# Earlier value casts, whole matmul pieces per step, earlier softmax sums and wider-spread exponentials in a fused attention and expert kernel

## The chip, the cores and the metric

One core of one Trainium2 chip. The metric is device time in microseconds (us) of one execution. Executions of one kernel mostly lie within 1% of each other; jobs run on different chips, so a variant is compared with the runs of the kernel before from its own job. Engines in the profile: PE is TensorE, PEld its weight loads, DVE VectorE, ACT ScalarE, POOL GpSimd, SP SyncE.

## The reference

Two parts. A linear attention over 8 batches, 8 heads, 576 tokens and 64 columns, whose result is 4608 tokens of 512 columns; then a mixture of experts that sends each token to the expert with the largest logit.

```python
def _attn_ref(q, k, v):
    q_s = softmax over the head columns of q          # cut: max, exp, sum, divide
    k_s = softmax over the tokens of k                # cut
    kv = np.einsum('bhsd,bhse->bhde', k_s, v)
    return np.einsum('bhsd,bhde->bhse', q_s, kv)

def _moe_ref(x, modality_id, w_gate, modality_bias, w1, w2):
    logits = x @ w_gate + modality_bias[modality_id]
    e_idx = np.argmax(logits, axis=1)
    gate_w = softmax(logits)[np.arange(N), e_idx]     # cut
    for e in range(E):
        mask = e_idx == e
        h = np.maximum(x[mask] @ w1[e], 0.0)
        out[mask] = gate_w[mask, None] * (h @ w2[e])
```

With these inputs the bias decides the expert, so tokens fall to two experts, one per modality. The kernel computes with those two and has a loop behind it for the case that they are not enough.

## The kernel before

Per batch, TensorE makes 36 kv matmuls from exp(k) and v, transposes exp(q), and makes the logits; VectorE turns the logits into an expert per token (the routing chain); matmuls with a permutation put the scaled tokens, sorted by expert, into `xs`. Between these small dependent steps TensorE is fed with *pieces* of the expert layers (the FFN): 8 matmuls of 256 columns (h) or 4 of 512 (y). The generator of a batch yields a number at each place where there is time for pieces, and `weave` hands them out; at some steps it also issues one ScalarE exponential or GpSimd cast of the next batch:

```python
def weave(side, rate, preps=(), at=()):
    owed = 0.0
    preps = iter(preps)
    for i, x in enumerate(side):
        if i in at:
            next(preps, None)          # one exponential or v cast of the next batch
        owed += x * rate
        while owed >= 1:
            mains(1)                   # one FFN piece
            owed -= 1
    alone(preps)
```

The end of the routing chain, with the softmax sums between the permutation and the scaling of the tokens:

```python
def route(b):
    ...                                 # logits, maximum, exp -> pr (ScalarE), isa, pos
    xps = [x_tile(b, 0)]
    yield 0.8
    xps.append(x_tile(b, 1))
    yield 1.6
    r_ps = ...                          # 2 matmuls with isa: ranks of the tokens
    ...                                 # aoff, pos
    nc.vector.tensor_tensor(out=perm, in0=iota_row.., in1=pos.., op=ALU.is_equal)
    ...
    gsum = small.tile([P, NT], FP32, name="gsum")
    nc.vector.reduce_sum(out=gsum, in_=pr, axis=AX.X)
    nc.vector.tensor_scalar_add(out=gsum, in0=gsum, scalar1=1e-9)
    nc.vector.reciprocal(out=gsum, in_=gsum)
    nc.vector.tensor_tensor(out=qi, in0=qi, in1=gsum.., op=ALU.mult)
    scale(0)                            # x_sb = x_ps * qi
    scale(1)
    yield 3.3
    ...                                 # xT: permutation matmuls, ScalarE copies into xs
```

The row numbers of the output are made by two routines: `slots(b)` makes the one-hot tiles `hlo` (VectorE) and `hv` (GpSimd by default), `places(b)` multiplies them (the `id` matmuls) and forms the row numbers `ix`. The results of an FFN piece go out by an indirect store on GpSimd's queue; the first ones are held until row numbers exist. The passage into batch 2, which the argument is about:

```python
    p2 = prep(2, nc.gpsimd)        # exp of k, casts of v (on GpSimd), exp of q, two steps each
    for i in range(6):
        mains(1)
        if i == 2:
            places(0)
            hold[0] = False
            store_held()           # the held stores enter GpSimd's queue here
        next(p2)

    def batch(b):
        side = chain(attend(b), route(b))
        for i, x in enumerate(side):
            if i == 0:
                slots(b - 1)
            if i == 5:
                places(b - 1)
            yield x
```

The softmax here doesn't subtract the row's maximum and nothing guards it: scores larger than these inputs give would overflow.

## Time and profile before

| | before |
|---|---|
| median (range) | 228.09 us (227.97 to 228.23), 3 runs |
| span of the profiled execution | 226.6 us |
| TensorE busy | 192.5 us, 85% |
| mean granted clock of TensorE | 0.971 |
| dearest wait of TensorE after the start | 3.5 us, for GpSimd's cast of batch 2's v |
| half clock in mid-span | 6.83 us, from 56.7 to 63.5 |

### The profile page before, as it was taken

The page shows a single profiled execution, that of the slowest core. Times are in us where ns is not written, and L with a number is a line of the kernel's source. Part 1 is how long each engine was busy: PE and PEld are TensorE (multiplying, and loading weights), DVE is VectorE, ACT ScalarE, POOL GpSimd, SP SyncE. Part 2 cuts the span into 40 slices and gives each one's busy share as a digit, 9 for nine tenths or more (in the row PEclk, how much of TensorE's full clock was granted, in tenths as well). Part 3 has the DMA queues.
Part 4 walks back from the last instruction along what each step waited for, and adds up shares of the span by engine and source line. Part 5 has one row for each costly group of instructions (what it writes and reads, how often), then busy time and mean ns, then how long its engine had stood idle before and what let it go on. Part 6 is the DMA issues. An engine that isn't in the chain of part 4 may idle for free.

```text
span 226.6 us, 5272 instructions
## 1 busy us (share of the span) xinstructions
PE 192.5 (85%) x1963; PEld 138.3 (61%) x1982; DVE 147.9 (65%) x499; ACT 150.9 (67%) x238; POOL 75.0 (33%) x86
## 2 busy tenths in 40 slices
PE   0287888985899998999999999999998999999940
PEld 0276775773666576567866876687677648476610
DVE  7788978986238784968687797868759766211100
ACT  3979698989173799489759958976553946244310
POOL 8910330004733461049015603810630071240350
PEclk9999999999589999999999999999999999999995
DMA  6999999999999949932983101120210022130220
GB/s 210 371 392 394 401 398 394 389 391 392 402 396 397 378 151 387 395 114 56 350 316 143 48 3 46 46 95 0 97 73 24 0 95 93 46 142 0 83 107 1
DMA packets 18953, 46.55 MB, mean 205 GB/s; under 512 B 1245, under 2 KB 1245, under 8 KB 18926
## 3 DMA queue, kind: packets, MB, share of 16 engines
q1 hardware_dynamic: 15936, 36.70, 43.7%
q0 software_dynamic: 2960, 9.44, 10.9%
q8 instruction: 16, 0.26, 0.5%
q14 instruction: 11, 0.09, 0.1%
q10 hardware_dynamic: 30, 0.05, 0.1%
HBM read 36.75 MB, written 9.70 MB: 205 GB/s over the span
## 4 chain that ended last, share of the span: by engine, by line
PE 61%; DVE 20%; ACT 5%; issue 4%; DMA 4%; POOL 1%; SPq 0%; POOLq 0%; ACTq 0%; DVEq 0%
PE y_ps L758 23%; PE h_ps L739 20%; PE xT_ps L631 4%; DMA st<-in_v_dram 4%; PE tp_ps L429 4%; PE x_ps L521 3%; PE kv_ps L392 3%; DVE lg L555 2%; PE lg_ps L491 2%; DVE x_sb L589 1%; ACT ek L374 1%; DVE lw L505 1%; DVE qi L503 1%; DVE perm L608 1%; PE id_ps L689 1%
## 5 line engine op out<-in xcount | busy, mean ns | idle before, releaser
L786 POOL DMA_INDIRECT out_dram<-y_sb,ix x37 | 37.0, 1000 | 127.5 <-DVE ix L703 32.9
L739 PE MATMUL h_ps<-xs,W 128*128 128x256 bf16 x576 | 70.0, 272 | 0.0
L758 PE MATMUL y_ps<-W,hT 128*128 128x512 bf16 x269 | 68.4, 383 | 1.8 <-ACT W L356 0.7
L739 PEld LDWEIGHTS <-W 128*128 128x128 bf16 x576 | 53.7, 98 | 7.1
L750 ACT ACTIVATE hT<-h_ps 128x512 bf16<-128x512 f32 x70 | 40.2, 605 | 13.0 <-PE h_ps L739 8.4
L644 ACT CAST xs<-xT_ps 128x512 f32 (+2 forms) x80 | 38.9, 556 | 8.3 <-PE xT_ps L631 7.8
L758 PEld LDWEIGHTS <-hT 128*128 128x128 bf16 x296 | 27.0, 98 | 26.4 <-issue 1.7
L589 DVE TENSOR_TENSOR x_sb<-x_ps,qi 128x512 bf16<-128x512 f32 (+1 forms) x40 | 26.2, 683 | 5.8 <-PE x_ps L521 5.3
L356 ACT COPY y_sb<-y_ps 128x512 f32<-128x512 f32 x22 | 13.0, 590 | 24.6 <-PE y_ps L758 23.8
L356 DVE COPY y_sb<-y_ps 128x512 f32<-128x512 f32 x14 | 9.7, 691 | 22.8 <-PE y_ps L758 18.9
L392 PE MATMUL kv_ps<-vb,ek 64*128 64x129 bf16 x288 | 12.7, 251 | 13.3 <-DVE vb L356 9.8
L392 PEld LDWEIGHTS <-ek 64*128 64x128 bf16 x288 | 10.7, 111 | 14.7 <-ACT ek L374 9.8
L374 ACT ACTIVATE ek<-st 128x1152 bf16<-128x1152 f32 x16 | 18.5, 1176 | 0.2 <-DMA st<-in_k_dram 0.2
L374 ACT ACTIVATE eq<-st 128x1152 bf16<-128x1152 f32 x16 | 18.2, 1190 | 0.1
L631 PEld LDWEIGHTS <-x_sb 128*128 128x128 bf16 (+1 forms) x160 | 11.0, 100 | 10.3 <-DVE x_sb L589 3.3
L521 PE MATMUL x_ps<-kvbd,et 128*128 128x128 bf16 (+1 forms) x160 | 16.9, 232 | 0.0
L631 PE MATMUL xT_ps<-perm,x_sb 128*128 128x128 bf16 (+1 forms) x160 | 15.3, 219 | 1.8 <-DVE x_sb L589 1.6
L429 PE MATMUL tp_ps<-ident,eq 128*128 128x128 bf16 x144 | 13.8, 243 | 0.7 <-ACT eq L374 0.5
L429 PEld LDWEIGHTS <-eq 128*128 128x128 bf16 x144 | 11.5, 112 | 3.8 <-issue 0.9
L356 POOL CAST vb<-st 128x1152 bf16<-128x1152 f32 x12 | 13.4, 1144 | 0.0
L521 PEld LDWEIGHTS <-et 128*128 128x128 bf16 (+1 forms) x160 | 11.4, 106 | 2.3 <-issue 1.7
L356 ACT COPY et<-tp_ps 128x1024 bf16<-128x1024 bf16 x7 | 7.2, 1028 | 6.2 <-PE tp_ps L429 6.1
(153 smaller groups left out, 219.3 us busy)
## 6 DMA issues: line engine op xcount, KB each, us to landing
st<-in_k_dram SPq DMA_DIRECT2D x8, 1152.0 KB, 12.8
st<-in_moe_w_dram SPq DMA_DIRECT2D x8, 1024.0 KB, 13.7
st<-in_v_dram SPq DMA_DIRECT2D x6, 1152.0 KB, 9.6
st<-in_q_dram SPq DMA_DIRECT2D x6, 1152.0 KB, 8.8
st<-in_v_dram SPq DMA_DIRECT2D x4, 576.0 KB, 8.0
st<-in_q_dram SPq DMA_DIRECT2D x4, 576.0 KB, 12.0
out_dram<-y_sb,ix POOLq DMA_INDIRECT x37, 3.3
W<-in_moe_modality_id_dram ACTq DMA_DIRECT2D x1, 36.0 KB
```

The costliest lines, as they stand in the source:

```text
L356: return (nc.scalar.copy if eng is nc.scalar else eng.tensor_copy)(out=out, in_=in_)
L374: nc.scalar.activation(out=view((eks if nm == "k" else eqs)[b], [[Dh, 2], [HG * Dh, NJ], [1, Dh]], 2 * g * Dh), in_=src[:, 2 * g : 2 * g + ...
L392: nc.tensor.matmul(out=kv[hg][:, 130 * hp : 130 * hp + 129], lhsT=ek[rows, j, P * hp : P * hp + P], rhs=vb[rows, j, hp, 0:129], start=(j = ...
L429: nc.tensor.transpose(out=view(tp[c0], [[2 * nj * 64, 2], [1, 64]], hp * nj * 64 + jj * 64), in_=eq[:, c0 + jj, P * hp : P * hp + P], iden ...
L521: nc.tensor.matmul(out=view(x_ps, [[2 * Dh, 2], [1, Dh]], (4 * (p_ % 2) + p_ // 2) * Dh, (0, T)), lhsT=et[:, p_, tcol[t] : tcol[t] + T], r ...
L589: scaled[b] = nc.vector.tensor_tensor(out=view(x_out[t], [[2 * Dh, HG], [Dh, 2], [1, Dh]], 0, (0, T)), in0=view(xps[t], [[2 * Dh, HG], [Dh ...
L631: nc.tensor.matmul(out=xT_ps[:, kd, 0:T], lhsT=x_out[t][0:T, kd * P : (kd + 1) * P], rhs=perm[0:T, t, 0:T], start=True, stop=True,)
L644: w = nc.scalar.copy(out=window(a + off, b, T, off > 0), in_=xT_ps[:, :, 0:T])
L739: nc.tensor.matmul(out=h_ps[:, f * w : (f + 1) * w], lhsT=w1(kd * F + (f0 + f) * P, P), rhs=x_in[:, kd, :], start=(kd == 0), stop=(kd == K ...
L750: nc.scalar.activation(out=h_out, in_=h_in, func=ACT.Relu)
L758: nc.tensor.matmul(out=y_ps, lhsT=hT[:, kf, t * P : (t + 1) * P], rhs=w2(kf * D, D), start=(kf == 0), stop=(kf == KF - 1),)
L786: store = nc.gpsimd.indirect_dma_start(out=out, out_offset=bass.IndirectOffsetOnAxis(ap=ix[0][:, t : t + 1], axis=0), in_=y_sb, in_offset= ...
```

## The change

Four parts. (1) *Casts first*: batch 2's v is cast on GpSimd ahead of the held stores, and the slot placement comes one piece later. (2) *Whole pieces*: all yields from batch 2 on are whole numbers, 16 pieces in each batch from 3 on instead of 15, with more of them inside the routing chain. (3) *Sums earlier*: the four softmax-sum operations go ahead of the x tiles. (4) *Spread*: the six exponentials and casts for the next batch are taken at other steps.

```diff
@@ passage into batch 2
         mains(1)
-        if i == 2:
+        next(p2)
+        if i == 3:
             places(0)
             hold[0] = False
             store_held()
-        next(p2)
@@ attend (several yields; three shown)
-        yield 0.8
+        yield 1 if b > 2 else 0
...
-            yield 1.2
+            yield 1
...
-        yield 1.4
+        yield 2
@@ route
+        if b > 1:
+            sums()                      # the four operations, now a function
         xps = [x_tile(b, 0)]
-        yield 0.8
+        yield 1 if b > 1 else 0.8
         xps.append(x_tile(b, 1))
-        yield 1.6
+        yield 2 if b > 1 else 1.6
...
-        nc.vector.reduce_sum(out=gsum, ...)      # and the three after it
+        if b < 2:
+            sums()
         scale(0)
         scale(1)
-        yield 3.3
+        yield 3 if b > 1 else 3.3
...
-            yield 0.7 if t < NT - 1 else 1
+            yield ((1, 0, 1, 1, 0)[t] if b > 1 else 0.7 if t < NT - 1 else 1)
@@ weave of the batches
-            (14 if b == 2 else 15.5) / 15.6,
+            1,
             prep(...),
-            (1, 2, 3, 4, 7, 8) if b > 2 else (4, 5, 8, 9, 17),
+            (1, 2, 3, 7, 8, 11) if b > 2 else (4, 5, 8, 9, 11, 12),
```

More of the change, by code (lines that the diff above doesn't have):

```diff
@@ L399, in attend @@
                 if j == 4:
-                    yield 0.2
+                    yield 0 if b > 1 else 0.2
             if hp == 0:
-                yield 0.2
+                yield 0 if b > 1 else 0.2
         kinv = small.tile([P, 2, 2], FP32, name="kinv")
@@ L478, in attend @@
                 if c0 == 4 and b > 1:
-                    yield 0.3
+                    yield 0
                     kvT = kv_turned()
-                    yield 0.7
+                    yield 1
                 elif nj > 1:
-                    yield 0.8
-        yield 0.8
+                    yield 1 if b > 2 else 0
+        yield 1
         if b != 1:
             g_of(kvT)
-            yield 1.2
+            yield 1
         lg_ps = sp_ps.tile([P, NT, NP, 18], FP32, name="lg_ps", tag="sp")
@@ L576, in route, with sums @@
         nc.vector.tensor_tensor(out=pos, in0=na, in1=cpos, op=ALU.mult)
+        gsum = small.tile([P, NT], FP32, name="gsum")
+        def sums():
+            nc.vector.reduce_sum(out=gsum, in_=pr, axis=AX.X)
+            nc.vector.tensor_scalar_add(out=gsum, in0=gsum, scalar1=1e-9)
+            nc.vector.reciprocal(out=gsum, in_=gsum)
+            nc.vector.tensor_tensor(out=qi, in0=qi, in1=view(gsum, [[1, NT], [0, H]]), op=ALU.mult)
+        if b > 1:
+            sums()
         xps = [x_tile(b, 0)]
-        yield 0.8
+        yield 1 if b > 1 else 0.8
         xps.append(x_tile(b, 1))
-        yield 1.6
+        yield 2 if b > 1 else 1.6
         r_ps = sp_ps.tile([P, 2, NT], FP32, name="r_ps", tag="sp")
@@ L617, in route @@
         )[1]
-        gsum = small.tile([P, NT], FP32, name="gsum")
-        nc.vector.reduce_sum(out=gsum, in_=pr, axis=AX.X)
-        nc.vector.tensor_scalar_add(out=gsum, in0=gsum, scalar1=1e-9)
-        nc.vector.reciprocal(out=gsum, in_=gsum)
-        nc.vector.tensor_tensor(out=qi, in0=qi, in1=view(gsum, [[1, NT], [0, H]]), op=ALU.mult)
+        if b < 2:
+            sums()
         scale(0)
         scale(1)
-        yield 3.3
+        yield 3 if b > 1 else 3.3
         free[0] = nc.vector
```

## The prediction

> **What bounds the kernel now.** I read the page first, then TensorE's time stage by stage, then who made it wait, then the order in time around the two dearest waits. The page's first part and its clock row:
>
> ```profile
> PE 192.5 (85%) x1963; PEld 138.3 (61%) x1982; DVE 147.9 (65%) x499; ACT 150.9 (67%) x238; POOL 75.0 (33%) x86
> ...
> PEclk9999999999589999999999999999999999999995
> ```
>
> TensorE (PE) carries the kernel: 192.5 of 226.6 us, against 151 and 148 for the next two. The row shows one dip of its clock in the middle, in slices 11 and 12. So what a change can win is TensorE's idle time and its time at half clock, no more. I cut the span into stages where each batch's 36 kv matmuls start (batch 2 at 57.46, 3 at 79.85, 4 at 101.29, and so on). Windows view, columns: window, length, busy us of PE, PEld, DVE, ACT, POOL, then clock, DMA share, GB/s:
>
> ```profile
> 50.80:53.97 3.17, 3.08 (x20) 1.85 (x22) 2.93 (x14) 3.17 (x6) 0.16 (x1) 1.00 1.05 391
> 53.97:57.46 3.49, 0.00 (x1) 0.02 (x2) 0.96 (x2) 3.25 (x4) 3.19 (x4) 0.89 1.06 392
> 57.46:63.50 6.04, 6.04 (x59) 4.32 (x59) 2.25 (x8) 0.23 (x1) 3.17 (x3) 0.50 1.05 406
> 79.85:101.29 21.44, 19.65 (x222) 14.23 (x225) 15.84 (x54) 17.05 (x29) 6.34 (x6) 1.00 0.74 271
> 101.29:121.35 20.06, 19.42 (x223) 14.17 (x226) 14.78 (x49) 16.14 (x28) 7.71 (x7) 1.00 0.61 221
> 121.35:140.97 19.62, 19.37 (x222) 14.16 (x225) 15.93 (x57) 15.93 (x28) 7.04 (x7) 1.00 0.14 53
> 160.57:180.60 20.03, 18.84 (x215) 13.87 (x218) 15.12 (x53) 11.47 (x24) 4.51 (x4) 1.00 0.14 54
> 188.00:217.60 29.60, 29.44 (x215) 19.59 (x214) 7.26 (x32) 12.49 (x21) 7.75 (x9) 1.00 0.18 70
> ```
>
> Batch 5 (121.35) is full: 0.25 us idle in 19.62. Batches 3 and 7 lose 1.8 and 1.2. The tail from 188 is full too. The great loss is 53.97 to 63.50: 3.49 us with nothing on TensorE, then 6.04 us at half clock, worth 3.0. TensorE's waits, columns: waiter, releaser, total us, times, longest:
>
> ```profile
> PE kv_ps L392 <- POOL vb L356: 3.5, 1, 3.5
> PE g_ps L453 <- ACT kvT L447: 1.6, 2, 1.1
> PE r_ps L582 <- DVE isa L570: 1.9, 2, 1.0
> PE id_ps L689 <- DVE hlo L679: 0.9, 1, 0.9
> PE tp_ps L429 <- ACT eq L374: 0.5, 1, 0.5
> PE id_ps L689 <- DVE ix L703: 0.4, 1, 0.4
> ```
>
> The 3.5 is GpSimd's (POOL) cast of batch 2's v. Its timeline tells why it is late, columns start, length, instruction, idle before:
>
> ```profile
> 53.81 1.16 POOL L786 DMA_INDIRECT out_dram<-y_sb,ix  x1 [23.56 <-DVE hi L662]
> 55.28 0.97 POOL L786 DMA_INDIRECT out_dram<-y_sb,ix  x1 [0.30 <-DVE hlo L679]
> 56.24 2.25 POOL L356 CAST vb<-st 128x1152 bf16<-128x1152 f32 x2
> ```
>
> GpSimd sat idle for 23.56 us on a store whose row numbers came only at 52.95, and the two casts stood behind two stores. The data was there: k of batch 2 was issued at 34.45 and took 12.8 us (47.3), the next k took 13.6 from 42.64 (56.2), and v, 1.18 MB at 392 GB/s or 3.0 us each, lies between: about 50.2.
>
> [...] half clock from 56.67 to 63.49 is 6.82 us, two windows, and it fell 2.7 us after the last matmul. [...] four y matmuls take 0.86 us in the chain of waits, 215 each[...].
>
> **The change part by part.** An FFN piece is 8 matmuls of 256 columns or 4 of 512, 0.87 us either way in the chain. The built program gives these orders.
>
> (1) Ahead of batch 2, the casts of v now come before the stores, and the slot placement one piece later. TensorE's order turns from 32 h, id, 8 h, 8 y, kv into 40 h, id, 8 y, kv. The fifth h piece waits for the eviction that starts at 49.29 (0.5), runs 49.8 to 50.7, and fills most of the 0.9 us wait for hlo. The 8 y then wait for a weight cast on VectorE until 51.83, run 51.9 to 53.65 (8 x 0.215), and kv starts there: its casts ran from 50.2 to 52.5, its k exponentials end at 52.4. 57.46 becomes 53.65: **3.8 us won**.
>
> (2) Batch 2 to batch 3. Before: 22.39 us with 14 pieces. Ideal: batch 5's 19.62 less 0.25 idle less one piece, 18.5. After it has 14 pieces too, at full clock, but with two new waits that I work out. kv ends at 54.8. The second exponential of q ends on ScalarE at 55.9 as before, so the transposes stand still from 55.05 to 55.95: 0.9. They end at 56.65, and then come the id matmuls, moved up by one piece; they need hv, which GpSimd builds after three stores: 53.81 to 54.97, 55.28 to 56.25, 56.55 to 57.5, then hv (1.16) to 58.7. Wait: 56.65 to 58.8, 2.15. With 0.2 for small ones: 18.5 + 3.25 = 21.75, **0.6 won**. Batch 3's kv starts at 75.4 instead of 79.85.
>
> (3) Batch 3. Before, both exponentials of its q ran after the x tiles (80.39 to 82.66), then k of the next batch, evictions and kvT behind them on ScalarE: 0.47 + 1.08 us of TensorE waits. Now they sit at two route steps of batch 2, beside y pieces. 21.44 plus one piece (16 instead of 15) is 22.3, against 19.37 + 0.87 = 20.25 ideal, say 20.5: **1.8 won**.
>
> (4) Batches 4 to 7 get 16 pieces each instead of 15, which only moves work from the tail (five pieces, 4.35 us each way), so it is worth what it fills. From lg the order is now 16 h, x, 8 h, x, 8 y, r: 2 x 0.87 + 0.33 + 0.87 + 0.33 + 1.73 = 5.0 us over the routing chain, which took 3.4 (lg end 109.75, isa end 113.14), where before it was 3.25. Then the softmax sums: four VectorE operations of 0.17 to 0.20, 0.75 together, go from between r and x_sb to before it; r to xT was 3.5 us (113.3 to 116.8), becomes 2.75, and 12 y cover 2.6. ScalarE in a batch: 16.0 us of 20, no new burst: at most one exponential (1.05) between two evictions, with three PSUM buffers. So: batch 4 20.06 + 0.87 - 20.5 = 0.4; batches 5 and 6 nothing; batch 7 0.6 of its 0.98 wait for isa; the 0.4 for ix after it. **1.4 won**.
>
> Sum: 3.8 + 0.6 + 1.8 + 1.4 = 7.6, so **220.5 us**. The drain after the last matmul, 217.6 to 226.6, stays.
>
> **The rivals.** (a) The new wait for hv halves the clock again: from 54.8 to 58.8 TensorE does only 0.95 us of transposes. [...] two half-clock windows cost 3 us: 223.5 to 224. For it: one window of 3.41 with 0.7 us of work (53.26 to 56.67) was enough. Against: on the same grid the next windows hold 1.5 us of work or more. One in five. (b) The gain of the casts is not 3.8 because v lands later, or GpSimd's wait is merely handed on: each us later is one us lost, up to 223. The DMA ran at 392 GB/s and nothing is moved ahead of v, so little speaks for it. (c) The work is only moved: TensorE is 85% busy, the whole pieces fill gaps of 0.2 us, and the gain is part 1 alone, 223 to 224. For it: batches 5 and 6 are full already. Against: the 1.08 and 0.98 waits are real. (d) More: hv's wait is shorter than I think, up to 218. Slower needs a new wait in each of five batches of more than 1.5 us; I found none in the order.
>
> **Range and chances.** 220.5, with (a) and (c) above and (d) below: 217.8 to 223.8 in 8 of 10. 2% is 223.5: faster 0.86, within 2% 0.13, slower 0.01.
>
> **What would show it.** Right: kv of batch 2 at about 53.7 with no idle over 1 us before it; no clock dip in mid-span; a wait of id for hv (GpSimd) of some 2 us near 57; batch 3 in 20.5 and equal batches after. Wrong: half clock anywhere from 57 to 67; a wait for v casts; batches of over 21 us, with TensorE waiting for ScalarE's evictions or x_sb.

## The result, and the profile after

The kernel after took 222.44 us in the median of four runs (222.01 to 222.57), against 228.04 for the kernel before (227.97 to 228.23; the three runs of the table above and one more). The ratio is 0.975, with a 95% interval of 0.9733 to 0.9767. Here and below a ratio is the one worked out from the fast runs of both kernels in the same job, so not quite the ratio of the medians quoted. The verdict is faster, by 5.6 us where 7.6 were predicted.

From the page of the kernel after, first its busy times, then the clock row:

```profile
PE 189.9 (86%) x1964; PEld 137.9 (62%) x1982; DVE 150.8 (68%) x502; ACT 150.4 (68%) x235; POOL 78.2 (35%) x86
...
PEclk9999769999699999999999999999999999999995
```

Two dips now. The one in slices 5 and 6 lies in the start-up, in code that the change does not touch; the mid-span one is shorter than before but still there. GpSimd is busy 3.2 us longer although it has the same 86 instructions: its stores take 1.9 of that (37.0 to 38.9) and its v casts 0.8. VectorE is busy 2.9 us longer. Its three more instructions, copies of `y_sb` that ScalarE did before, take 2.1; beyond them one `hlo` and one weight cast take 1.9 more, which matters below, and the `ix` operations 1.3 less.

The windows view of the kernel after (window, length, busy us of PE, PEld, DVE, ACT, POOL, then clock, DMA share, GB/s), cut where the run of h matmuls ahead of batch 2 starts and then where each batch's kv matmuls start:

```profile
47.03:52.40 5.37, 4.71 (x43) 3.81 (x40) 4.80 (x12) 5.12 (x7) 1.97 (x2) 1.00 1.05 391
52.40:57.38 4.98, 3.24 (x12) 1.17 (x15) 4.74 (x16) 2.87 (x4) 2.02 (x2) 0.81 1.06 392
57.38:78.22 20.84, 19.20 (x199) 12.93 (x202) 13.14 (x45) 14.41 (x23) 9.86 (x10) 0.96 1.05 398
78.22:98.44 20.22, 19.98 (x225) 14.70 (x226) 15.65 (x53) 16.46 (x29) 8.09 (x7) 1.00 0.87 318
98.44:118.48 20.04, 19.93 (x226) 14.63 (x227) 15.64 (x53) 16.14 (x28) 8.11 (x7) 1.00 0.66 231
```

From batch 3 on the batches are equal (batches 5 and 6 take 20.03 each), about 20.1 us with 16 pieces and about 0.1 to 0.25 us idle. That is what parts 2 to 4 promised. But kv of batch 2 starts at 57.38, where the kernel before had 57.46 and the prediction 53.65. TensorE's waits in the kernel after (waiter, releaser, total us, times, longest):

```profile
PE xT_ps L638 <- DVE x_sb L599: 2.2, 2, 2.0
PE y_ps L765 <- DVE W L356: 1.6, 1, 1.6
PE id_ps L696 <- POOL hv L679: 1.5, 2, 1.1
PE id_ps L696 <- DVE hlo L686: 0.8, 1, 0.8
```

The 3.5 us for GpSimd's v cast and the waits for kvT are gone. In their place stand a wait for a weight cast on VectorE, one for `hlo` on VectorE and the one for `hv` on GpSimd. (The 2.0 for `x_sb` is in the start-up, before batch 2.) The order in time, for the kernel before (start, length, instruction):

```profile
49.96 0.82 DVE L679 TENSOR_TENSOR hlo<-iota_row,lo 128x640 bf16<-128x640 bf16 x1
50.70 1.22 DVE L356 CAST W<-st 128x2048 bf16<-128x2048 f32 x1
```

and for the kernel after, in the same place:

```profile
50.43 3.05 POOL L356 CAST vb<-st 128x1152 bf16<-128x1152 f32 x2 [20.14 <-DMA st<-in_v_dram]
50.71 1.76 DVE L686 TENSOR_TENSOR hlo<-iota_row,lo 128x640 bf16<-128x640 bf16 x1
52.40 2.17 DVE L356 CAST W<-st 128x2048 bf16<-128x2048 f32 x1
52.53 0.53 PE L696 MATMUL id_ps<-hv,hlo 64*128 64x114 bf16 x5 [0.79 <-DVE hlo L686]
54.62 2.83 PE L765 MATMUL y_ps<-W,hT 128*128 128x512 bf16 x7 [1.56 <-DVE W L356]
57.38 1.88 PE L392 MATMUL kv_ps<-vb,ek 64*128 64x129 bf16 x36
61.40 0.52 PE L696 MATMUL id_ps<-hv,hlo 64*128 64x114 bf16 x5 [1.14 <-POOL hv L679]
```

The same `hlo` took 0.82 before and 1.76 after; the same weight cast 1.22 and 2.17; the two v casts 2.25 and 3.05. They overlap in time only in the kernel after. Neither engine's instruction changed, only what ran on the other one meanwhile.

The lengths fit instructions that took turns, by an estimate worked out from the two traces: each next instruction is taken from the end of the one before it on either engine, with the duration that it has alone in the kernel before. In a narrower timeline the first v cast ends at 51.80. From there come `hlo` 0.82, to 52.6 (trace: 52.47), the second v cast 1.12 (half of 2.25), to 53.6 (trace: 53.48), and the weight cast 1.22, to 54.7 (trace: 54.57): right to within 0.15 us. It does not hold for every pair: VectorE's `hv` ran beside the first v cast until 50.80 and took 0.75, as in the kernel before, and that cast took 1.37 against 1.12. By what means the two engines hold each other up is not shown.

Last, the clock. Windows view of the kernel after, at the edges of the dip:

```profile
52.06:55.47 3.41, 1.33 (x8) 0.72 (x10) 3.31 (x8) 3.21 (x5) 1.42 (x1) 1.00 1.06 393
55.47:58.88 3.41, 3.41 (x35) 1.96 (x35) 1.96 (x10) 1.40 (x2) 2.13 (x2) 0.50 1.05 390
```

The 3.41 us ahead of the dip hold both new waits and 1.33 us of matmuls; then TensorE ran 3.41 us at half clock, in which most of the y and kv matmuls lie. The dips of these two traces last 3.41 or 6.83 us, and in the kernel after the start-up dip ends at 31.58 and this one begins at 55.47, 23.89 us later, seven times 3.413: a stretch of 3.41 us between two such points is called a window here.

The gain by stretches, from the starts of the same instructions in the two traces. Batches 3 to 6 of the kernel before have 15 pieces, so one piece of 0.87 us is added to each to compare like with like. (Batch 3 is 21.37 us between the starts of its own kv matmuls and the next; the prediction's 21.44 takes its end, 101.29, from the chain that ended last.)

| stretch | before | after | won | predicted |
|---|---|---|---|---|
| up to the h run ahead of batch 2 | 46.27 | 47.03 | -0.76 | 0 |
| h run to kv of batch 2 | 11.19 | 10.35 | 0.84 | 3.8 |
| kv of batch 2 to kv of batch 3 | 22.39 | 20.84 | 1.55 | 0.6 |
| batch 3 (one piece added) | 22.24 | 20.22 | 2.0 | 1.8 |
| batches 4 to 6 (three pieces added), and on to the last matmul (four taken off) | | | 2.1 | 1.4 |
| sum | | | 5.7 | 7.6 |

The -0.76 belongs to the start-up dip (24.75 to 31.58). Of the 14 traces five have two windows of half clock near 24 to 32 us, in code that is the same in all but one kernel; the kernel after had it in this trace and not in its second one below. With it this trace has three half-clock windows before the last matmul, 10.2 us, in which by half the speed up to 5.1 us were lost, 2.3% of 222.

### The profile page after: what moved, and what is told of

It reads as the page before. It is cut to its first block, busy times and chain, and to the rows that moved or that the text cites.

```text
span 220.9 us, 5278 instructions
## 1 busy us (share of the span) xinstructions
PE 189.9 (86%) x1964; PEld 137.9 (62%) x1982; DVE 150.8 (68%) x502; ACT 150.4 (68%) x235; POOL 78.2 (35%) x86
## 4 chain that ended last, share of the span: by engine, by line
PE 76%; DVE 12%; DMA 4%; issue 2%; POOL 1%; SPq 0%; ACT 0%; POOLq 0%; DVEq 0%; ACTq 0%
PE y_ps L765 28%; PE h_ps L746 27%; PE tp_ps L429 5%; PE x_ps L521 4%; PE xT_ps L638 4%; DMA st<-in_v_dram 4%; PE kv_ps L392 3%; PE lg_ps L491 2%; PE id_ps L696 1%; DVE x_sb L599 1%; DVE kvbd L413 1%; DVE W L356 1%; PE kvT_ps L445 1%; DVE hlo L686 1%; DVE perm L618 1%
## 5 line engine op out<-in xcount | busy, mean ns | idle before, releaser
L793 POOL DMA_INDIRECT out_dram<-y_sb,ix x37 | 38.9, 1052 | 98.9 <-ACT y_sb L356 50.5
L757 ACT ACTIVATE hT<-h_ps 128x512 bf16<-128x512 f32 x70 | 41.0, 598 | 14.5 <-PE h_ps L746 14.0
L651 ACT CAST xs<-xT_ps 128x512 f32 (+2 forms) x80 | 38.0, 569 | 11.9 <-PE xT_ps L638 11.8
L356 ACT COPY y_sb<-y_ps 128x512 f32<-128x512 f32 x19 | 11.1, 585 | 23.4 <-PE y_ps L765 20.8
L356 DVE COPY y_sb<-y_ps 128x512 f32<-128x512 f32 x17 | 11.7, 691 | 20.1 <-PE y_ps L765 20.1
L356 POOL CAST vb<-st 128x1152 bf16<-128x1152 f32 x12 | 14.2, 1211 | 20.1 <-DMA st<-in_v_dram 20.1
L392 PE MATMUL kv_ps<-vb,ek 64*128 64x129 bf16 x288 | 11.4, 237 | 10.2 <-POOL id_i L194 10.2
L392 PEld LDWEIGHTS <-ek 64*128 64x128 bf16 x288 | 9.6, 104 | 11.5 <-issue 11.0
L679 POOL TENSOR_TENSOR hv<-hhi,vals 128x570 bf16<-128x570 bf16 x7 | 10.5, 1500 | 1.3 <-DVE hhi L675 0.6
```

The lines of the kernel that those rows point to most:

```text
L356: return (nc.scalar.copy if eng is nc.scalar else eng.tensor_copy)(out=out, in_=in_)
L392: nc.tensor.matmul(out=kv[hg][:, 130 * hp : 130 * hp + 129], lhsT=ek[rows, j, P * hp : P * hp + P], rhs=vb[rows, j, hp, 0:129], start=(j = ...
L651: w = nc.scalar.copy(out=window(a + off, b, T, off > 0), in_=xT_ps[:, :, 0:T])
L757: nc.scalar.activation(out=h_out, in_=h_in, func=ACT.Relu)
L793: store = nc.gpsimd.indirect_dma_start(out=out, out_offset=bass.IndirectOffsetOnAxis(ap=ix[0][:, t : t + 1], axis=0), in_=y_sb, in_offset= ...
```

## The experiments

All twelve gave the right result. The theory after the traces: parts 2 to 4 do what was predicted, and part 1 fails because GpSimd's casts, moved early, collide with VectorE's `hlo` and weight cast, and the clock then falls. The rival: the casts are innocent, and the time went to the later placement of the slots, or to the stores.

**The casts part alone, on the kernel before.**

```diff
+        next(p2)
-        if i == 2:
+        if i == 3:
             places(0); hold[0] = False; store_held()
-        next(p2)
```

> The kernel before with the first part of the change alone: casts of batch 2's v ahead of the stores, slot placement one piece later. The prediction's step 1 (3.8 us, and with step 2 4.4) expects 223.6 us. My theory after the changed kernel's trace, that the early GpSimd casts hold up VectorE's hlo and weight cast beside them (0.82 to 1.76 us, 1.22 to 2.17 us) so that kv starts hardly earlier, expects hlo and the weight cast as long as in the changed kernel, and 225.5 to 226.5 us. If the part is worth nothing: 228.

Measured: 225.46 us, ratio 0.9941 (0.9911 to 0.9971) to 226.54 before: 1.3 us by the ratio, far from 3.8. In this execution `hlo` started at 50.17, ahead of the v casts at 50.42, and took 0.82, against the expectation; the weight cast behind it took 2.17 and the two v casts 3.67. kv of batch 2 starts 8.5 us after the h run (7.4 predicted). Then the id matmuls wait 2.5 us for `hv`, and the clock is at half from 60.65 to 64.06. So part 1 alone is worth little, and its gain is lost at two places.

**Everything but the casts part.**

```diff
 # the kernel after, with the loop ahead of batch 2 as before
-        next(p2)
-        if i == 3:
+        if i == 2:
             ...
+        next(p2)
```

> The changed kernel with the first part undone: whole-piece steps, softmax sums ahead and spread exponentials stay. My theory from the stages of the changed kernel (2.1 us in batch 3, 2.0 in batches 4 to 7 and the end) expects 223.8 to 224.5 us, with the 3.5 us wait for the v cast and two half-clock windows still there. The prediction's steps 3 and 4 (3.2 us) expect 224.9.

Measured: 222.36 us, ratio 0.9813 (0.9786 to 0.9839). The 3.5 us wait for v is still there, with one half-clock window behind it and not the two expected; batches 4 on take 20.03. Parts 2 to 4 thus carry most of the gain, 1.9%, and by the ratios part 1 adds 0.3 to 0.6% to it (0.9784 and 0.975 for the kernel after in its two jobs). In the traces it adds nothing: from the h run to kv of batch 3 this kernel takes 31.20 us (46.78 to 77.98) and the kernel after 31.19 (47.03 to 78.22). What part 1 wins ahead of batch 2 is lost within it.

**The v cast of batch 2 on VectorE.** It takes the early casts off GpSimd, so that none of them runs beside `hlo` and the weight cast, and leaves the rest of the change.

```diff
-    p2 = prep(2, nc.gpsimd)
+    p2 = prep(2, nc.vector)
```

> The changed kernel with the two casts of batch 2's v on VectorE behind the weight cast, GpSimd free until the stores. Theory (GpSimd's casts slow VectorE): hlo back at 0.8 us, weight cast at 1.2, kv of batch 2 starts 2.5 to 3 us earlier against the 40 h than in the changed kernel (10.35 us after their start there); the id matmuls then wait 2 to 3 us for hv, so 220.5 to 222 us. Rival (the slow VectorE operations have another cause, such as the loads arriving): hlo 1.7 and the weight cast 2.1 stay, 222.4 or slower.

Measured: 221.78 us, ratio 0.9794 (0.9765 to 0.9824). Its order in time:

```profile
49.59 0.82 DVE L686 TENSOR_TENSOR hlo<-iota_row,lo 128x640 bf16<-128x640 bf16 x1
50.32 1.22 DVE L356 CAST W<-st 128x2048 bf16<-128x2048 f32 x1
...
53.43 1.20 PE L392 MATMUL kv_ps<-vb,ek 64*128 64x129 bf16 x36
...
59.71 0.75 PE L696 MATMUL id_ps<-hv,hlo 64*128 64x114 bf16 x5 [2.87 <-POOL hv L679]
```

With no GpSimd cast beside them both VectorE operations are back at their old lengths, and kv starts 7.5 us after the h run (45.91), as step 1 of the prediction worked it out. And yet the total hardly moved: the three microseconds came back as a wait of 2.87 us for `hv` and a half-clock window from 59.4 to 62.8. The collision is the cause of step 1's failure, but removing it alone wins nothing clear of noise, because the next wait stands right behind.

**Dummy casts.** The converse: the kernel before, with two more GpSimd casts of the same shape, which nothing needs, ahead of its stores.

```diff
         if i == 2:
+            for g in range(2):
+                nc.gpsimd.tensor_copy(out=<vb of the other buffer>, in_=<the staged v of batch 2>)
             places(0)
```

> The kernel before with two more casts of batch 2's v on GpSimd, ahead of the stores, into a buffer that is overwritten before it is read; nothing else moves. Theory: they run from about 50.3 on, hlo goes from 0.82 to about 1.7 us and the weight cast from 1.22 to about 2.1, the stores and the true casts come about 2 us later, 229.5 to 230.5 us. Rival (another cause): hlo 0.82 and the weight cast 1.22 stay, 228.0 us.

Measured: 228.32 us, 1.8 above the 226.54 of before by the medians, ratio 1.0057 (1.0033 to 1.0082).

```profile
50.48 3.06 POOL L961 CAST vb<-st 128x1152 bf16<-128x1152 f32 x2 [20.13 <-DMA st<-in_v_dram]
50.77 1.76 DVE L679 TENSOR_TENSOR hlo<-iota_row,lo 128x640 bf16<-128x640 bf16 x1
52.45 2.17 DVE L356 CAST W<-st 128x2048 bf16<-128x2048 f32 x1
```

With the placement where it always was, `hlo` goes to 1.76 and the weight cast to 2.17, the very lengths of the kernel after. The rival that blames the later placement falls: the cast on the other engine suffices.

**The kernel after again,** in another job on another chip.

> The changed kernel as it is, on the chip of the next three, so that they can be compared with it: 0.975 to 0.982 of the kernel before.

Measured: 222.86 us, ratio 0.9784 (0.9736 to 0.9832) to 227.82. The trace went the other way from the first one:

```profile
49.73 0.82 DVE L686 TENSOR_TENSOR hlo<-iota_row,lo 128x640 bf16<-128x640 bf16 x1
50.44 3.24 POOL L356 CAST vb<-st 128x1152 bf16<-128x1152 f32 x2 [20.17 <-DMA st<-in_v_dram]
...
54.56 1.20 PE L392 MATMUL kv_ps<-vb,ek 64*128 64x129 bf16 x36
...
60.13 0.74 PE L696 MATMUL id_ps<-hv,hlo 64*128 64x114 bf16 x5 [2.93 <-POOL hv L679]
```

No start-up dip, so the h run began at 46.05 and `hlo` 0.7 us ahead of the v casts; it was not held up. v lands near 50.4 in both traces, so a microsecond in the start-up decides which of the two starts first. kv came 8.5 us after the h run instead of 10.35, but then the id matmuls waited 2.93 us instead of 1.14, and the clock was at half for two windows, 59.45 to 66.27, instead of one. The weight cast beside the v casts still took 2.20. The loss changes its place; the total is much the same.

**The stores behind `hv`, with v on VectorE.** If the wait for `hv` behind three stores is what holds the gain, sending the held stores after `hv` of batch 1 must free it.

```diff
 # on top of the v cast on VectorE
         if i == 3:
             places(0)
-            hold[0] = False
-            store_held()
...
             if i == 0:
                 slots(b - 1)              # issues hv
+                if b == 2:
+                    hold[0] = False
+                    store_held()
```

> The casts of batch 2's v on VectorE, and the three held stores on GpSimd behind hv of batch 1 instead of ahead of it. Theory: the id matmuls' wait for hv (2.87 us with the casts on VectorE and the stores ahead) shrinks to under 0.5, and with it the near-idle stretch that halves the clock: no half-clock window after 50 us, 2.5 to 4 us below the changed kernel, about 219 if the kernel before is at 228. Rival (the wait is merely handed on to kvT, the exponentials or the clock): within 1 us of the changed kernel.

Measured: 220.27 us, ratio 0.9658 (0.9623 to 0.9693). The waits for `hv` are down to 0.4 us in all, and there is no half clock after 50 us in this trace until the last matmuls are done. That is 1.4% more than the v cast on VectorE alone (0.9794; another job, but the intervals are apart).

**The softmax sums back in their old place.**

```diff
-        if b > 1:
-            sums()
         xps = [x_tile(b, 0)]
 ...
-        if b < 2:
-            sums()
+        sums()
```

> The changed kernel with the four softmax-sum operations back between perm and x_sb. The prediction's working (r to x_sb 3.5 us against 2.6 us of y pieces) expects TensorE to wait some 0.8 us for x_sb in each of six batches: 3 to 4.8 us slower than the changed kernel. Rival (another wait, r for isa, would have taken the time anyway): less than 1 us slower.

Measured: 224.67 us, ratio 0.9873 (0.9837 to 0.9909), 1.8 us above the kernel after of the same job, and less than expected. Its row in TensorE's waits:

```profile
PE xT_ps L635 <- DVE x_sb L597: 4.2, 8, 2.0
```

Eight waits instead of the kernel after's two; the long one of 2.0 is again in the start-up, and six batches have 0.33 us each, and a batch takes 20.43 us instead of 20.03. So the sums are worth 0.4 us a batch.

**The exponentials at their old steps.**

```diff
-            (1, 2, 3, 7, 8, 11) if b > 2 else (4, 5, 8, 9, 11, 12),
+            (1, 2, 3, 4, 7, 8) if b > 2 else (4, 5, 8, 9, 17),
```

> The changed kernel with the exponentials at the old steps. Theory: the burst of two q exponentials at the start of batch 3 is back (0.5 + 1.1 us of waits), and in later batches two k exponentials come together but ScalarE has room: 1.2 to 2 us slower. Rival (the whole-piece steps alone removed the waits): no slower than 0.5 us.

Measured: 224.26 us, ratio 0.9865 (0.9821 to 0.9909), 1.4 above the kernel after of the same job, as expected. Where it goes, in order of time:

```profile
80.33 0.40 PE L429 MATMUL tp_ps<-ident,eq 128*128 128x128 bf16 x4 [0.26 <-ACT eq L374]
...
81.38 0.40 PE L429 MATMUL tp_ps<-ident,eq 128*128 128x128 bf16 x4 [0.65 <-ACT eq L374]
```

Batch 3's transposes wait for its own q exponentials, and the batch takes 21.67 us instead of the 20.04 of the kernel after in the same job. It is the late pair of step 3 of the prediction, and it is needed only once, since from batch 4 on the exponentials were in time already.

**Junk matmuls at the two waits.** The kernel after with TensorE kept busy while it waits, to see what the half clock alone costs.

```diff
             places(0)
+            busy(16)                      # 16 matmuls whose result nobody reads
             hold[0] = False
...
             if i == 5:
+                if b == 2:
+                    busy(24)
                 places(b - 1)
```

> The changed kernel with idle TensorE kept busy ahead of batch 2: 16 matmuls on constants (0.9 us) in the wait for the weight cast, 24 (1.3 us) in the wait for hv. Theory: near-idle windows there halve the clock in every trace of the changed kernel so far (one or two windows of 3.41 us, each worth 1.7): no half clock between 50 and 70 us, 1 to 2.5 us below the changed kernel, 0.968 to 0.974 of the kernel before. Rival (the halved clock covers waits for other engines and costs nothing): 0.976 to 0.982, as the changed kernel.

Measured: 221.34 us, ratio 0.974 (0.9717 to 0.9764), at the edge of what was expected. No half clock between 50 and 70 us any more, in spite of waits of 0.8, 0.7 and 0.9 us that remain. All ten traces with the stores ahead of `hv` and without these junk matmuls have a half-clock window between 54 and 67 us, and this one has none: that supports, with one trace, that the clock falls for want of work. What the clock alone costs is not shown. The ratio is 0.1 and 0.4% below those of the kernel after in its two jobs, and the intervals overlap.

**Whole pieces alone, on the kernel before.**

```diff
 # all yields and the rate as in the kernel after; loop, sums and steps of the exponentials as before
```

> The kernel before with the whole-piece steps and the 16 pieces per batch alone. By what is left when casts (1.1 us alone), sums (1.8) and spread exponentials (1.4) are taken from the 5 us of the whole: 0.7 to 1.5 us below the kernel before, 0.993 to 0.997. Rival (the steps carry the change and the others only tune it): 2.5 us or more, 0.989 or less.

Measured: 226.33 us, ratio 0.9966 (0.9942 to 0.9989), as expected. The batches take 20.43 us with a wait for `x_sb` of 0.3 in each. Whole pieces alone are worth 0.3%; the sums and the spread on top of them pay 1.5% more (0.9966 to the 0.9813 of the kernel without the casts part, from another job). Whether these two would pay as much without the whole pieces was not tested.

**The stores behind `hv`, and nothing else,** v still on GpSimd: the edit of the run with the stores behind `hv`, without the move of v to VectorE.

```diff
 # on the kernel after
         if i == 3:
             places(0)
-            hold[0] = False
-            store_held()
...
                 slots(b - 1)
+                if b == 2:
+                    hold[0] = False
+                    store_held()
```

> The changed kernel with only the three held stores behind hv of batch 1; batch 2's v stays on GpSimd beside VectorE's weight cast. Theory: the weight cast still takes 2.1 us and kv is as late as in the changed kernel, but the wait for hv goes: 1 to 2 us below the changed kernel, 0.970 to 0.974. Rival (stores and casts must both move): 0.976 or more; if the stores are all of it: 0.966.

Measured: 218.88 us, ratio 0.9662 (0.9622 to 0.9702): better than expected, at the value put down for "if the stores are all of it", and equal to the version with v on VectorE (0.9658). Its order in time:

```profile
55.06 1.20 PE L392 MATMUL kv_ps<-vb,ek 64*128 64x129 bf16 x36
...
55.93 1.58 POOL L679 TENSOR_TENSOR hv<-hhi,vals 128x570 bf16<-128x570 bf16 x1 [1.75 <-DVE hhi L675]
...
57.64 0.53 PE L696 MATMUL id_ps<-hv,hlo 64*128 64x114 bf16 x5
...
58.47 1.19 POOL L793 DMA_INDIRECT out_dram<-y_sb,ix  x1 [0.95 <-DVE kinv L409]
```

and the clock row of its page:

```profile
PEclk9999999999999999999999999999999999999995
```

The collision is still there (weight cast 2.17, y waits 1.47, kv 8.5 us after the h run), but `hv` now runs before the stores and is ready when the transposes end, so the wait of 2.9 is gone and with it, in this trace, the half clock. Two of the six runs took 220.6 and 220.9 us at a granted clock of 0.961, the others 218.4 to 219.0 at 0.984 or more, so dips still come in some executions. Of the two losses in the passage into batch 2, the stores ahead of `hv` were the binding one.

**The best version:** stores behind `hv`, v on VectorE, and 16 junk matmuls over a wait in the start-up, ahead of the first weight casts.

```diff
 # on the kernel with the stores behind hv and v on VectorE
     a1 = attend(1)
     steps(a1, 4)
+    busy(16)
     cast_weights(0, 0, nc.gpsimd)
```

> Casts on VectorE and stores behind hv, and 16 matmuls on constants in TensorE's 1.0 to 2.0 us wait for the first x_sb near 23 us, where four traces of ten show two half-clock windows. Theory: they no longer come, 0.3 to 0.5 us on average below the version without them (0.966 of before): 0.962 to 0.966. Rival (the phase of the windows decides alone): half clock there again, 0.966 or more.

Measured: 218.12 us (217.94 to 219.86, six runs), ratio 0.9631 (0.9597 to 0.9665) to 227.22, with no half clock before the end in the profiled execution. Two of the six runs took 219.7 and 219.9 us at a granted clock of 0.978, the other four about 218.1 at 0.985 or more. The difference of 1.7 us is what one half-clock window of 3.41 costs at most (half of it); where it fell isn't known. The kernel beats both others: 9 us under the one before and, by the ratios, 1.2% or more under the one after. Its lead over the last run is within both intervals, so the junk matmuls' own share is not shown. Nor does one trace without the start-up dip: eight of the 13 traces without these matmuls have none either.

## Why the prediction was right or wrong

The time was in the range and on the right side of 2%, but of its four steps the first failed, and the gain was made elsewhere: steps 2 to 4 gave 5.6 us where 3.8 were predicted. That this made up for 1.8 of the 3.0 us missing from step 1 is luck, and without it the time (about 224.2) would have been outside the range. Of the prediction's own signs, kv at 53.7 and a clock without a dip did not come; the wait for `hv` and the even batches did.

- **Step 1, casts first: 3.8 us predicted, 0.84 measured.** The step that failed is "its casts ran from 50.2 to 52.5" together with "The 8 y then wait for a weight cast on VectorE until 51.83": both take durations from a trace in which GpSimd was idle beside VectorE, and use them where the two run together. The missing 3.0 us are 0.28 of a longer h run (4.71 for 4.43), 0.79 of waiting for `hlo`, 0.89 more of waiting for the weight cast (1.56 for 0.67) and 1.01 for the 8 y, of which most ran at half clock (2.76 for 1.75). The VectorE variant shows that without the collision the step's 7.4 us come out at 7.5; the dummy casts show the collision by itself. In the second trace, where only the weight cast was held up, step 1 gave 2.7 (8.5 against 11.19), and step 2 lost 2.2 (24.59 against 22.39).
- **Step 2: 21.75 us predicted, 20.84 measured.** The wait for `hv` behind three stores was predicted as 2.15 us; it was 1.14 in the first trace, since kv came late, and 2.5 to 2.9 in the four traces with the stores still ahead in which kv came within 8.5 us of the h run. The mechanism was right. The 0.9 more than predicted is not a new gain: kv was late by more than that, and what came late waited less. Steps 1 and 2 together gave 2.4 instead of 4.4.
- **Step 3, batch 3: 1.8 predicted, 2.0 measured.** Right; the run with the old steps finds the late exponentials exactly there.
- **Step 4, batches 4 to 7: 1.4 predicted, 2.1 measured.** The sum hides terms that were wrong both ways. Batch 4 was put at 0.4 and "batches 5 and 6 nothing"; they gained 0.9, 0.45 and 0.45. Batch 7 and its wait for `ix` were put at 1.0; from its kv to the last matmul only about 0.3 was won. Batches 5 and 6 fitted a 16th piece into 0.41 us more than it had taken with 15 (19.62 to 20.03). Without the early sums it takes 20.43, so it is the sums that hide the piece, also where the profile before showed only 0.25 us of idle time.
- **Rival (a), a second half clock, one in five:** a dip came in both traces of the kernel after, but only in the second one behind the wait for `hv` (2.93 us); in the first one (55.4 to 58.9) it came ahead of that wait, behind those for `hlo` and the weight cast. The argument against it, that "the next windows hold 1.5 us of work or more", was too hopeful: 1.33 us of plain matmuls in 3.41, in two bursts behind waits of 0.79 and 1.56, did not keep the clock. Rival (b), that GpSimd's wait is merely handed on, was right in its outcome, for another reason than it gave first: v landed on time, at 50.4. Rival (c), all the gain from part 1, is the reverse of what the runs showed. The start-up dip, 0.76 us of chance against the change, was in no step.

Open: how much work in a window keeps the clock (in the trace of the kernel after the two windows ahead of its dips hold 1.33 us each, and the one from 58.88 to 62.29, with 2.18, was followed by full clock); and why the kernel before differs by over a microsecond between jobs, where only the chip is known to differ and the granted clocks overlap (0.963 to 0.978 at a median of 226.54 us, 0.969 to 0.983 at 227.82).

## What to carry to other kernels

When an instruction moves on GpSimd, look at what VectorE runs beside its new place before using its old duration, and the other way round: here a GpSimd cast beside them added 0.94 us to a VectorE operation of 0.82 (`hlo`) and 0.95 to a weight cast of 1.22. Follow an engine's queue past the wait you remove, because the next thing in it (here `hv` behind the stores, waited for up to 2.93 us) may give the whole gain back; moving that as well was worth more than the planned move. Filling a chain with whole pieces of other work won only 0.3% by itself here; more came with the earlier sums and the spread exponentials on top of it.
